# Where the load buffers of a one-token attention kernel start in SBUF, and which queue loads x

## The chip, the cores and the metric

The kernel runs on one core of one Trainium2 chip. The metric is device time in microseconds (us) of that core. A time is the median of several executions; nearly all executions of one kernel here agree within 0.1%. Each run of an experiment was timed beside executions of the kernel before on the same chip.

## The reference, cut to what matters

One token x of 640 values goes through a layer norm, a query projection, attention over a cache of 32,768 positions in 32 heads of 192, an output projection and a small ReLU MLP, all in bf16:

```python
q = (ln(x) @ wq).reshape(1, 1, 32, 192)           # wq: 640 x 6144
scores = einsum("bhqd,bhkd->bhqk", q, k_cache) * 192 ** -0.5
o = einsum("bhqk,bhkd->bhqd", softmax(scores), v_cache)
h = x + o.reshape(1, 1, 6144) @ wo                # then h + MLP(ln(h))
```

Keys and values are 403 MB each. Every byte is used once, so the kernel is a stream of loads with arithmetic beside it.

## The kernel before

SyncE issues every load. A key or value tile is 128 partitions with one contiguous row of 64 x 192 bf16 = 24,576 B each (3 MB in all); there are four key places and two value places, loaded in turn: key, value, key, value. A value load waits until PE has read the place (`PV`).

```python
def sbuf(name, shape, dtype):
    return ctx.enter_context(nc.sbuf_tensor(name, shape, dtype))
...
kt = [sbuf(f"kt{i}", [P, JL * Dh], bf16) for i in range(NL)]    # 4 x 24,576 B a partition
vt = [sbuf(f"vt{i}", [P, JL * Dh], bf16) for i in range(NV)]    # 2 x 24,576 B
wq_s = sbuf("wq_s", [P, DT * QG * Dh], bf16)                    # 15,360 B, rows of 3,072 B
wq_h = sbuf("wq_h", [P, DT, Dh], bf16)
wo_s = sbuf("wo_s", [P, 3, D], bf16)                            # rows of 3,840 B
...
def dma_program(g):                                             # SyncE
    ...
    load(x_row[:], A_x.rearrange("b s (c p) -> (b s c) p", p=P), "dx", "x")
    load(wq_v, wq_view[:, :, 0:QG * Dh], "dwq", "wq", 0)
    for h in range(H):
        for ld in range(NL if h < LAST else NL - 1):
            n = NL * h + ld
            load(kt[ld][:], rows(k_hd, h, P * JL * ld, JL), f"dk{ld}", "k", h, ld)
            if n >= NV:
                hp, lp = divmod(n - NV, NL)
                g.wait("PV", hp, 2 * lp + 1)
            load(vt[ld % NV][:], rows(v_hd, h, P * JL * ld, JL), f"dv{ld % NV}", "v", h, ld)
            # wq for the next eight heads, wo for the next two: at some h, ld
            ...
```

The allocator gives addresses in order, so each tile starts where the one before it ends.

The softmax here doesn't subtract the row's maximum and nothing guards it: scores larger than these inputs give would overflow.

## Time and profile before

| | |
|---|---|
| time | 1944.24 us (3 runs, 1944.11 to 1944.43) |
| span of the profiled run | 1941.3 us |
| bytes read from HBM | 825 MB |

The page cuts the span into 40 slices. A row of digits gives the busy share in each, in tenths, and the row GB/s gives what the 16 DMA engines moved. The trace also holds one record for each DMA packet, with its size and the time that it took. In this kernel a packet is one row of one partition; an engine serves 8 of the 128 rows of a load. These records are read from the trace file itself, since the usual views show only their sums. The *usual time* of a size is the time that the most packets of that size take; a packet that takes longer is called *late*.

### The profile page before, as it was taken

How to read it: one execution, taken by the hardware profiler on the slowest of the kernel's cores; microseconds unless marked ns; L12 is line 12 of the kernel's file. 1: busy time of each engine (PE TensorE's matmuls, PEld its weight loads, DVE VectorE, ACT ScalarE, POOL GpSimd, SP SyncE). 2: the span in 40 equal slices, each digit the busy share in tenths (PEclk: the TensorE clock that was granted, in tenths of full speed). 3: DMA queues.
4: the chain of work that ended last, by engine and by line, in shares of the span. 5: the costliest groups of instructions: out<-in, count | busy, mean ns of one | idle time of the engine just before them, and what ended most of it. 6: DMA issues, size and time to landing. Idle time of an engine off the chain costs nothing.

```text
span 1941.3 us, 36397 instructions
## 1 busy us (share of the span) xinstructions
PE 1601.3 (82%) x16098; PEld 1112.5 (57%) x16098; DVE 1590.4 (82%) x924; ACT 998.3 (51%) x2064; POOL 0.7 (0%) x6
## 2 busy tenths in 40 slices
PE   5887888787887888887788878888888888888887
PEld 3555555555555565655556556555555556565555
DVE  6888888887888888887888878888778888888886
ACT  4555545554455555455455555545445555554544
POOL 0000000000000000000000000000000000000000
PEclk9889889888898888888888988888888888888988
DMA  9999999999999999999999999999999999999997
GB/s 403 428 429 431 430 429 431 430 429 431 429 431 429 432 429 431 431 430 428 427 429 430 429 428 429 431 428 430 426 420 432 429 429 431 426 430 427 430 427 299
DMA packets 44814, 825.44 MB, mean 425 GB/s; under 512 B 4580, under 2 KB 6116, under 8 KB 12132
## 3 DMA queue, kind: packets, MB, share of 16 engines
q1 hardware_dynamic: 44772, 824.99, 99.6%
q8 instruction: 13, 0.21, 0.0%
q14 instruction: 29, 0.24, 0.0%
HBM read 824.97 MB, written 0.00 MB: 425 GB/s over the span
## 4 chain that ended last, share of the span: by engine, by line
DMA 76%; PE 22%; SPq 1%; issue 1%; ACT 0%; DVE 0%; POOLq 0%
DMA kt<-in_A_k_cache_dram 76%; PE o_ps L303 11%; PE tp L322 10%; SPq L210 1%; PE mm L303 1%; PE sp L303 0%; ACT kT L509 0%; POOLq L285 0%; DVE o_pair L620 0%; PE attT L303 0%; ACT pB L515 0%; PE mm L498 0%; ACT sd_ln L549 0%; DVE xn_ln L641 0%; DVE y_row L671 0%
## 5 line engine op out<-in xcount | busy, mean ns | idle before, releaser
L602 DVE TENSOR_TENSOR pr<-kt,qb 128x1536 f32<-128x1536 bf16 (+1 forms) x384 | 775.3, 2019 | 273.1 <-DMA kt<-in_A_k_cache_dram 259.1
L509 ACT COPY kT<-tp 128x1024 bf16<-128x1024 bf16 (+1 forms) x900 | 819.4, 990 | 324.0 <-PE tp L322 322.8
L322 PE MATMUL tp<-ident_f,kt 128*128 128x128 f32 x3462 | 572.0, 332 | 309.3 <-POOLq L285 308.9
L605 DVE TENSOR_REDUCE sc<-pr 128x8 f32<-128x1536 f32 (+1 forms) x384 | 773.9, 2015 | 13.3
L322 PEld LDWEIGHTS tp<-ident_f,kt 128*128 128x128 f32 x3462 | 498.7, 173 | 326.4 <-POOLq L285 324.3
L303 PE MATMUL o_ps<-vt,pB 128*2 128x384 bf16 x2286 | 468.1, 356 | 5.9 <-POOLq L285 5.9
L303 PE MATMUL o_ps<-vt,pA 128*2 128x384 bf16 x1778 | 330.8, 326 | 0.0
L303 PEld LDWEIGHTS o_ps<-vt,pB 128*2 128x2 bf16 x2286 | 183.4, 89 | 240.8 <-issue 82.4
L515 ACT ACTIVATE pB<-sp 128x20 bf16<-128x20 f32 (+2 forms) x258 | 48.1, 186 | 481.4 <-PE sp L303 481.4
L303 PEld LDWEIGHTS sp<-qm,kT 128*128 128x128 bf16 x6924 | 193.4, 97 | 83.6 <-issue 59.2
L303 PEld LDWEIGHTS o_ps<-vt,pA 128*2 128x2 bf16 x1778 | 150.6, 85 | 144.6 <-issue 7.9
L303 PE MATMUL sp<-qm,kT 128*128 128x2 bf16 x6924 | 212.1, 164 | 7.4 <-ACT kT L509 2.7
L524 ACT ACTIVATE pA<-sc 128x12 bf16<-128x12 f32 (+2 forms) x257 | 53.5, 208 | 113.6 <-DVE sc L605 112.2
L515 ACT ACTIVATION_READ_ACCUMULATOR pB<-sp 128x1 f32 x258 | 50.2, 195 | 0.0
L524 ACT ACTIVATION_READ_ACCUMULATOR pA<-sc 128x1 f32 x257 | 48.7, 190 | 0.0
L303 PE MATMUL mm<-ident_f,o_pair 2*128 2x1 f32 x384 | 47.8, 247 | 1.0 <-DVE o_pair L620 1.0
L303 PEld LDWEIGHTS mm<-ident_f,o_pair 2*128 2x128 f32 x384 | 45.1, 186 | 1.9 <-DVE o_pair L620 1.4
L610 DVE TENSOR_REDUCE rec<-mm 128x1 f32<-128x20 f32 x32 | 5.7, 179 | 46.3 <-PE mm L303 45.2
L532 ACT COPY wq_h<-wq_s 128x960 bf16<-128x960 bf16 x32 | 31.4, 980 | 2.9 <-DMA wq_s<-in_A_wq_dram 2.9
L620 DVE TENSOR_SCALAR o_pair<-o_ps,rec 2x384 f32<-2x384 f32 x32 | 28.4, 889 | 2.8 <-PE o_ps L303 1.7
L303 PE MATMUL mm<-wq_h,xn_ln 128*1 128x192 bf16 x160 | 18.7, 248 | 4.8 <-ACT wq_h L532 4.8
L303 PE MATMUL attT<-oT,wo_s 128*128 128x1 bf16 x465 | 15.9, 163 | 0.3 <-DVE oT L625 0.3
(65 smaller groups left out, 150.7 us busy)
## 6 DMA issues: line engine op xcount, KB each, us to landing
kt<-in_A_k_cache_dram SPq DMA_DIRECT2D x127, 3072.0 KB, 22.7
vt<-in_A_v_cache_dram SPq DMA_DIRECT2D x127, 3072.0 KB, 15.7
wq_s<-in_A_wq_dram SPq DMA_DIRECT2D x4, 1920.0 KB, 20.3
wo_s<-in_A_wo_dram SPq DMA_DIRECT2D x16, 480.0 KB, 17.0
kt<-in_A_k_cache_dram SPq DMA_DIRECT2D x1, 1920.0 KB, 19.9
kt<-in_A_v_cache_dram SPq DMA_DIRECT2D x2, 960.0 KB, 24.6
kt<-in_B_w_dram SPq DMA_DIRECT2D x1, 1920.0 KB, 20.3
wq_s<-in_B_w_dram SPq DMA_DIRECT2D x1, 960.0 KB, 22.2
```

What stands on the lines that cost most here:

```text
L210: g.do(lambda: nc.sync.dma_start(out=dst, in_=src), sem, label, by=16)
L303: return lambda: pe.matmul(o, lhsT=w, rhs=r, **kw)
L322: calls.append(lambda b=b, o=o: pe.transpose(out=dst[:, b, :], in_=src[:, o:o + 2 * P].bitcast(f32), identity=ident_f[:]))
L509: g.do(lambda: act.copy(out=kT[c % 2][:, b0:b0 + nb, :], in_=src[:, 0:nb, :].bitcast(bf16)), "act_pe", ("cp", h, c, k))
L515: g.do(lambda: act.activation(out=pB[c % 4][:, 0:jp], in_=sp[:, 0:jp], func=F.Exp, scale=SCALE, accum_out=dsums[:, 2 * c + 1:2 * c + 2]), ...
L524: g.do(lambda: act.activation(out=pA[c % 4][:, 0:jd], in_=sc[c % 4][:, 0:jd], func=F.Exp, scale=SCALE, accum_out=dsums[:, 2 * c:2 * c + 1] ...
L532: g.do(lambda: act.copy(out=wq_h[:], in_=wq_v[:, :, hh * Dh:(hh + 1) * Dh]), "act_pe", ("wqh", h))
L602: g.chain(lambda: dve.tensor_tensor(out=pr[:, 0:j1 - j0, :], in0=src[:, (off + j0) * Dh:(off + j1) * Dh].rearrange("p (j d) -> p j d", d=D ...
L605: red = lambda: dve.reduce_sum(out=sc[c % 4][:, j0:j1], in_=pr[:, 0:j1 - j0, :], axis=X)
L610: g.chain(lambda: dve.reduce_sum(out=rec[:, 0:1], in_=mm[:, 0:2 * NCM], axis=X), "dve_act")
L620: g.do(lambda: dve.tensor_scalar_mul(out=dst, in0=src, scalar1=rec[0:2, 1:2]), "dve_pe", ("os", h))
```

## The change

The intent: let the long rows land at multiples of 512 B, so that no row starts or ends within a block, and take the small load of x out of SyncE's queue so that the stream starts earlier.

```diff
-    def sbuf(name, shape, dtype):
-        return ctx.enter_context(nc.sbuf_tensor(name, shape, dtype))
+    def sbuf(name, shape, dtype, align=32):
+        return ctx.enter_context(nc.sbuf_tensor(name, shape, dtype, align_bytes=align))
@@
-    kt = [sbuf(f"kt{i}", [P, JL * Dh], bf16) for i in range(NL)]
-    vt = [sbuf(f"vt{i}", [P, JL * Dh], bf16) for i in range(NV)]
-    wq_s = sbuf("wq_s", [P, DT * QG * Dh], bf16)
+    kt = [sbuf(f"kt{i}", [P, JL * Dh], bf16, 512) for i in range(NL)]
+    vt = [sbuf(f"vt{i}", [P, JL * Dh], bf16, 512) for i in range(NV)]
+    wq_s = sbuf("wq_s", [P, DT * QG * Dh], bf16, 512)
     wq_h = sbuf("wq_h", [P, DT, Dh], bf16)
-    wo_s = sbuf("wo_s", [P, 3, D], bf16)
+    wo_s = sbuf("wo_s", [P, 3, D], bf16, 512)
@@ dma_program
-        load(x_row[:], A_x.rearrange("b s (c p) -> (b s c) p", p=P), "dx", "x")
@@ act_program
+        g.do(lambda: act.dma_start(out=x_row[:], in_=A_x.rearrange("b s (c p) -> (b s c) p", p=P)), "dx", ("x",), by=16)
```

## The prediction

> **What bounds the kernel now.** I read the slices and the queue table of the page first, to see whether one unit is full all the time.
>
> ```profile
> DMA  9999999999999999999999999999999999999997
> GB/s 403 428 429 431 430 429 431 430 429 431 429 431 429 432 429 431 431 430 428 427 429 430 429 428 429 431 428 430 426 420 432 429 429 431 426 430 427 430 427 299
> DMA packets 44814, 825.44 MB, mean 425 GB/s; under 512 B 4580, under 2 KB 6116, under 8 KB 12132
> q1 hardware_dynamic: 44772, 824.99, 99.6%
> ...
> DMA 76%; PE 22%; SPq 1%; issue 1%; ACT 0%; DVE 0%; POOLq 0%
> ```
>
> The 16 DMA engines are full in every slice but the last, and one queue, SyncE's, does 99.6% of it. The rate stands at 426 to 432 GB/s from slice 2 to slice 39, with one dip to 420. PE and VectorE are each busy for 82% of the span; they wait for data. Next came the stretches, to rule out a stage with another limit, and then the queue's own waits, because the chain of waits gives PE 22% and that had to be understood.
>
> ```profile
> 250.00:500.00 250.00, 205.73 (x2028) 143.15 (x2028) 204.64 (x115) 128.19 (x265) 0.00 (x0) 0.86 1.01 430
> 500.00:1000.00 500.00, 416.35 (x4181) 289.90 (x4181) 415.69 (x238) 257.12 (x533) 0.00 (x0) 0.87 1.00 430
> 1000.00:1500.00 500.00, 414.61 (x4156) 287.73 (x4155) 412.32 (x233) 258.31 (x536) 0.00 (x0) 0.88 1.00 429
> 1900.00:1941.00 41.00, 32.99 (x412) 23.58 (x412) 24.20 (x26) 18.52 (x43) 0.00 (x0) 0.83 0.70 278
> ```
>
> ```profile
> SPq L210 <- PE o_ps L303: 1343.1, 95, 33.9
> SPq L210 <- PE mm L303: 454.4, 31, 18.2
> ```
>
> SyncE's sequencer waits for PE for 1343 us in all (a value buffer must be read before it is filled again), yet the DMA share of the stretches stays 1.00. So these waits are back-pressure, not lost time: a 3 MB value load takes 7.3 us of the engines (3,145,728 bytes at 430 GB/s) and lands 15.7 us after its issue (median of the page's issue table), so some 8.4 us of work are still queued ahead of it when it goes out. The 22% of PE in the chain are the stretches in which the chain steps through such a release; no faster PE would shorten them.
>
> Last came the two ends, from the timeline and the chain in order of time.
>
> ```profile
> 0.96 0.38 SPq L210 DMA_DIRECT2D x_row<-in_A_x_dram  x1
> 1.40 0.40 SPq L210 DMA_DIRECT2D wq_s<-in_A_wq_dram  x1
> ...
> 8.90 0.99 ACT L532 COPY wq_h<-wq_s 128x960 bf16<-128x960 bf16 x1 [2.86 <-DMA wq_s<-in_A_wq_dram]
> ...
> 12.06 0.32 ACT L540 CAST qb<-mm 128x192 bf16<-128x192 f32 x1 [0.72 <-PE mm L303]
> 16.21 2.56 DVE L602 TENSOR_TENSOR pr<-kt,qb 128x2304 f32<-128x2304 bf16 x1 [9.65 <-DMA kt<-in_A_k_cache_dram]
> ```
>
> ```profile
> 1892.02 19.93 DMA kt<-in_A_k_cache_dram
> 1911.95 0.04 issue
> 1911.99 1.20 PE tp L322 x9
> ```
>
> At the start, [...]the query is ready at 12.4 us, 3.8 us before the first key tile lands. At the end, the last key pieces are waited for at 1912 us; from there to 1938 us the chain is compute on PE, ScalarE and VectorE, which no placement of buffers shortens. So the span is the stream of loads up to 1912 us, plus about 29 us.
>
> **What the Trainium skill says.** (1) "DMA: Bandwidth & Descriptors", section "Where 436 GB/s comes from": 16 ports of 32 B at 850 MHz are 435.2 GB/s. The trace runs at 430, which agrees and leaves 1.2% at the very most to win in the stream. (2) The same page, "How a descriptor splits into AXI transactions": a descriptor that doesn't start at a multiple of 256 B gets one more transaction, and the bytes skipped in the first one still cost 32-byte beats. This is the one statement that gives the change a mechanism; the trace speaks against its costing anything here, see below. (3) The same page, "Issuing engines are not separate DMA queues": issuing from several engines saves only the sequencer's time to issue. The trace has that time: 0.44 us. (4) "SBUF — State Buffer", "Operand start alignment" says that element-aligned places are legal and that its runs timed nothing; so it gives no speed either way.
>
> **The change part by part.**
> *Where things lie.* A 16,384-byte scratch and four 32-byte constants come first, so kt0 lies at byte 16,512 = 32 x 512 + 128. A kt or vt place is 24,576 B = 48 x 512, so all six places and wq_s (163,968) lie at 128 past a multiple of 512 (and of 256). After wq_s come 1,920 B of wq_h, which put wo_s at 181,248 = 354 x 512: wo_s is at a multiple of 512 already. After the change all are. The parts of the last head inside kt0 and kt1 start at multiples of 512 within their tile, so they follow. HBM rows of keys and values are 24,576 B long and contiguous, and don't change. That wo_s is aligned before is luck: it is a control inside the present trace.
>
> *What alignment could save.* From the trace's packet records (size and time taken), the usual time of a packet of each size is: 1,280 B 55 ns, 3,072 B 121, 6,144 B 234, 7,680 B 291, 15,360 B 573, 24,576 B 912; these all go to misaligned places. The wo rows, 3,840 B, to an aligned one: 149 (1,935 of 2,048 packets). By the skill's figure a beat is 1/0.85 = 1.18 ns. Packets minus their bare beats leave: 55-47.1 = 7.9, 121-112.9 = 8.1, 234-225.9 = 8.1, 291-282.4 = 8.6, 573-564.7 = 8.3, 912-903.5 = 8.5 ns misaligned; and 149-141.2 = 7.8 ns aligned. If the shift by 128 B cost 4 beats (4.7 ns), the aligned packet should leave about 3.5 ns. It leaves what the others leave, within 0.1 to 0.8 ns. So I take alignment to be worth 0 ns a packet in the main case. The check of scale: 8 packets of 912 ns and a semaphore write of 9 ns make 7.31 us a load, 430 GB/s, which is the plateau; packets run back to back and this is the whole cost.
>
> *x on the ScalarE queue.* SyncE drops one issue: 1.40 - 0.96 = 0.44 us earlier for wq and everything after, if ScalarE's issue doesn't hold up SyncE's. The stream is full from there to the end, so the shift arrives whole at the end: 0.44 us. ScalarE gains an issue of about 0.4 us before its first table load (0.91 to 2.19 now); its next work is at 5.74, so this is hidden. x itself is five packets of 256 B, 15 ns each.
>
> Sum: 1944.24 - 0 - 0.44 = 1943.8. Allowing the smaller chance of a gain its weight, I say 1943.5.
>
> **The rivals.**
> *A. The skill's beats are real at the write side.* Each of the 32,512 packets of 24,576 B saves 4.7 ns: 32,512 x 4.7 / 16 = 9.6 us; the smaller misaligned packets (3,456 + 256 + 256 + 128, and up to 1,536 of 1,280 B) add 4,096 x 4.7 / 16 = 1.2 to 1.7 us. With x: 1944.2 - 11.5 = 1932.8, 0.6% faster. For it: the cost of misalignment is stated on a page, and the room (8.5 ns over bare beats a packet, 17.3 us in all) is there. Against it: the aligned wo rows. The control isn't perfect, since 3,840 is 7.5 x 512 and a half block at its end may cost what the others lose by their start. I give A, or a part of it over 0.3%, 13%.
> *B. The time is in the stragglers.* The 24,576 B packets average 917.7 ns, not 912; the longest took 2,724 ns. The surplus over 912 is 11.5 us of the engines' time. If writes to whole 512 B blocks thin the stragglers, some of this comes back: 2 to 6 us. Nothing in the profile ties stragglers to a place, and a cause at the HBM side is as good; 7%, partly inside A.
> *C. A second queue costs something.* The two issues could be served one after the other, and then the 0.44 us shrink to nothing; x could also land late. The query has 3.8 us of slack, so lateness is hidden. Time: 1944.2. Added set-up for another queue might make 1944.5 to 1945.
> *D. A faster stream meets PE.* Only if A holds: PE and VectorE at 82% have room for 0.6%, so no new bound.
>
> **Range and chances.** Main case with and without C: 1943.4 to 1944.6, about four in five. A full A lies outside the range I give, a half A or B inside it: 1937 to 1945. More than 2% faster would need 39 us, more than twice the 17.3 us that packets spend beyond bare beats; more than 2% slower would need packets of 930 ns for no reason that I see. Faster 1%, within 2% 98%, slower 1%.
>
> **What would show it right or wrong.** The usual packet of 24,576 B: 912 ns means no effect, 907 means A. The plateau: 430 means none, 432 to 433 means A. The wo packet should stay at 149. The first wq issue should stand near 0.96 instead of 1.40 us, with x issued by ScalarE's sequencer beside it; the first key wait should end near 15.8 us instead of 16.2. The tail from the last key wait to the end should stay 29 us. The prediction is wrong if aligned long packets are faster than 910 ns, if the stragglers' 11.5 us fall by half, or if the stream shows a gap.

## The result, and the profile after

The changed kernel takes 1933.82 us (4 runs, 1932.93 to 1934.0) against 1944.17 us of the kernel before (4 runs, 1943.9 to 1944.43). The ratio is 0.9946, with a 95% interval of 0.9929 to 0.9963. That is 0.5% or 10.3 us faster: far within the 2% that count as "same", and outside the range that I gave (1937 to 1945).

The slices, queues and the chain of waits of the changed kernel, from its page:

```profile
DMA  9999999999999999999999999999999999999997
GB/s 404 432 431 434 432 432 433 432 431 434 431 433 432 433 432 432 433 432 431 433 432 432 433 430 432 432 430 426 429 432 433 430 429 432 429 427 428 433 431 298
q1 hardware_dynamic: 44762, 824.99, 99.6%
...
q10 hardware_dynamic: 10, 0.00, 0.0%
...
DMA 76%; PE 22%; SPq 1%; issue 0%; ACT 0%; DVE 0%; POOLq 0%
```

The kernel is bound by the same thing as before: DMA full, PE 22% of the chain. The plateau moved from about 430 to about 432 GB/s. The stretches (length; busy us and count of PE, its weight loads, VectorE, ScalarE, GpSimd; granted clock, DMA share, GB/s) say the same:

```profile
250.00:500.00 250.00, 206.06 (x2063) 144.04 (x2064) 204.80 (x118) 128.06 (x267) 0.00 (x0) 0.86 1.01 432
500.00:1000.00 500.00, 420.71 (x4189) 292.17 (x4188) 417.86 (x237) 259.27 (x537) 0.00 (x0) 0.87 1.00 432
1000.00:1500.00 500.00, 415.57 (x4202) 288.13 (x4201) 416.40 (x235) 262.64 (x541) 0.00 (x0) 0.89 1.00 431
```

SyncE's waits for PE are as long as they were, as back-pressure has to be:

```profile
SPq L210 <- PE o_ps L302: 1327.7, 95, 34.0
```

The two ends, from the timeline of the changed kernel:

```profile
0.91 0.56 ACTq L552 DMA_DIRECT2D x_row<-in_A_x_dram  x1
...
0.97 0.45 SPq L210 DMA_DIRECT2D wq_s<-in_A_wq_dram  x1
...
15.96 2.56 DVE L602 TENSOR_TENSOR pr<-kt,qb 128x2304 f32<-128x2304 bf16 x1 [9.40 <-DMA kt<-in_A_k_cache_dram]
```

```profile
1902.65 1.18 PE L321 MATMUL tp<-ident_f,kt 128*128 128x128 f32 x9
```

wq goes out 0.43 us earlier, and the first key is worked on 0.25 us earlier. The transposes of the last key pieces, which started at 1911.99 us, start at 1902.65; from there to the end of the span it is 29.1 us, after 29.3 before. So the time came out of the stream.

The packet records say where. For each kernel, over its 32,512 packets of 24,576 B: the share at exactly 912 ns; the mean; what the packets take above 912 ns, summed over all and divided by 16 engines, once for those up to 40 ns late (the *spread*) and once for those more than 40 ns late (the *stragglers*, with their number); and the time of all packets of the loads over 16 engines.

```
             at 912   mean ns   spread us   stragglers, us    all loads us
before        0.43     917.7      5.50        324, 6.05          1930.3
after         0.99     913.7      0.06        162, 3.40          1921.2
```

The usual packet didn't change: 912 ns. But before, only 43% of them took it; 56% took 913 to 929 ns, and 1% longer. After, 99% take 912. The same is true of the short rows: 1,280 B takes 55 ns in 33% of the packets before and in all of them after; 3,072 B takes 121 ns in 39% and in 99%. All packets together fall by 9.1 us: 5.4 from the spread of the long ones, 2.7 from their stragglers, 1.0 from the shorter rows. The stream starts 0.39 us earlier (its first packet at 2.08 instead of 2.46 us). Together that is 9.5 of the 9.6 us by which the span of the profiled runs fell.

### The profile page after: what moved, and what is told of

It is laid out like the page before. It is cut to its first block, busy times and chain, and to the rows that moved or that the text cites. A ratio compares the mean times of both kernels' runs of the same rounds, so it can differ in the third digit from the quotient of the medians.

```text
span 1931.7 us, 36397 instructions
## 1 busy us (share of the span) xinstructions
PE 1602.2 (83%) x16098; PEld 1113.3 (58%) x16098; DVE 1590.0 (82%) x924; ACT 998.5 (52%) x2064; POOL 0.7 (0%) x6
## 4 chain that ended last, share of the span: by engine, by line
DMA 76%; PE 22%; SPq 1%; issue 0%; ACT 0%; DVE 0%; POOLq 0%
DMA kt<-in_A_k_cache_dram 76%; PE o_ps L302 11%; PE tp L321 10%; SPq L210 1%; PE mm L302 1%; PE sp L302 0%; ACT kT L508 0%; POOLq L284 0%; DVE o_pair L620 0%; PE attT L302 0%; ACT pB L514 0%; PE mm L497 0%; ACT sd_ln L548 0%; DVE xn_ln L641 0%; DVE y_row L671 0%
```

## The experiments

Eleven kernels ran. The table has the packets of nine of them; the sections explain them. "Offset" is the start of the key and value rows past a multiple of 512 B. "Loads alone" are kernels that do nothing but load and then write zeros, so their output is wrong. Two more of these, dma_runs (1921.60 us) and dma_offsets (1926.79 us), change the offset on the way and have their own section.

```
             start of keys, values (mod 512)   at 912   mean ns   spread us   stragglers, us   time us   same chip, before
x_only        128                                0.40     917.8      5.71        271, 6.14      1943.48     1944.11
align_only    0                                  0.99     914.0      0.10        194, 3.98      1933.80     1944.11
off256        256                                0.99     913.6      0.11        181, 3.14      1934.22     1944.11
off32         32                                 0.13     919.4      8.32        310, 6.72      1947.61     1944.11
off64         64                                 0.21     918.1      6.49        317, 5.94      1945.70     1943.66
keys_only     keys 0, values 128                 0.97     914.5      0.28        269, 4.71      1935.06     1943.66
page4k        0 (mod 4096)                       0.99     913.7      0.08        145, 3.34      1933.32     1944.19
dma_off128    128, loads alone                   0.20     915.5      7.03          2, 0.05      1928.37     1943.66
dma_off0      0, loads alone                     1.00     912.1      0.03         13, 0.08      1919.13     1943.66
```

After the first look at the trace I held that the placement does it, by removing the spread (theory P), against the shift by the second queue (rival X) and the skill's extra beats, whose mark, a usual packet of 907 ns, the trace lacked.

### x_only: the queue alone

```diff
 # kernel before
-        load(x_row[:], A_x...., "dx", "x")                        # SyncE
+        g.do(lambda: act.dma_start(out=x_row[:], in_=A_x....), "dx", ("x",), by=16)   # first in act_program
```

> Only x moves to the ScalarE queue; all places stay at 128 past a multiple of 512 B. Theory P (placement makes the gain, by taking away the spread of 0 to 14 ns that two thirds of the misaligned packets show above their usual time): 1943.8 us, 0.4 us faster than before at most; the share of 24,576 B packets at exactly 912 ns stays near 0.43. Rival X (the shift of the stream by the second queue makes the gain): near 1934 us, share near 0.99.

It took 1943.48 us against 1944.11; ratio 0.9997 (0.9984 to 1.0011). The spread stayed. The medians differ by 0.6 us; the interval holds zero and ends at 3 us, far from 10. Rival X falls. (The "two thirds" of the expectation is too high: 57% of the long packets were late before.)

### align_only: the placement alone

```diff
 # changed kernel
+        load(x_row[:], A_x...., "dx", "x")                        # back on SyncE, first
-        g.do(lambda: act.dma_start(out=x_row[:], ...), "dx", ("x",), by=16)
```

> Only the places move to multiples of 512 B; x stays first on the SyncE queue. Theory P: 1934.2 us, that is the changed kernel plus 0.2 to 0.4 us, with the share of 24,576 B packets at 912 ns near 0.99 and their usual time still 912, not 907. Rival X: near 1944 us. If the skill's beats were the cause, the usual time would be 907 ns; after the changed kernel's trace I expect that no more.

It took 1933.80 us; ratio 0.9948 (0.9934 to 0.9962), the whole effect, with a usual packet of 912 ns. Theory P stands. The gap to the changed kernel (1933.82, another chip) is nothing, so x on ScalarE doesn't show beside it.

### off256 and off32: which boundary, and how the cost grows

```diff
 # kernel before
+    sbuf("pad", [P, 64], bf16)        # off256: 128 B; off32: 416 B
     kt = [sbuf(f"kt{i}", [P, JL * Dh], bf16) for i in range(NL)]
```

> All places moved by 128 B, so keys, values and wq start at 256 past a multiple of 512, and wo at 128; x on SyncE. Theory P256 (the boundary that counts is 256 B, the size of the transactions that the skill names): as align_only, 1934.5 us, share of long packets at 912 ns near 0.99; the wo packets, now at 128, lose their uniform 149 ns (share from 0.95 or 1.00 to about 0.4), worth 0.4 us. Theory P512 (the boundary is 512 B): as before, 1944 us, share near 0.43.

> All places moved by 416 B, so keys, values and wq start at 32 past a multiple of 512, wo at 416; x on SyncE. Theory E (any start off the boundary costs the same, a partial piece at each end of the row): as before, 1944 us, share at 912 ns near 0.43, spread worth about 2.7 ns a packet. Theory B (the cost is the extra 32-byte beats: 4 at offset 128, 1 at offset 32): a quarter of the spread, 0.7 ns a packet, 1936 to 1937 us.

Offset 256 took 1934.22 us (ratio 0.9949, 0.9936 to 0.9963), the same as offset 0, so the boundary that counts is 256 B and not 512. The stretches of the run with offset 256 and of the run with offset 32:

```profile
500.00:1000.00 500.00, 418.18 (x4226) 289.99 (x4224) 418.20 (x239) 259.11 (x539) 0.00 (x0) 0.88 1.00 432
```

```profile
500.00:1000.00 500.00, 420.09 (x4193) 291.68 (x4191) 414.77 (x237) 257.79 (x535) 0.00 (x0) 0.87 1.00 429
```

Offset 32 is the slowest of all: 1947.61 us (1.0019, 1.0005 to 1.0033). Its usual packet takes 915 ns, and its spread is 8.3 us where offset 128 has 5.5. Counting skipped beats, it should have cost a quarter. So theory B, the prediction's rival A in another form, falls, though it had named nearly the right time; and theory E, the same cost for every offset, falls too.

One part of the expectation for offset 256 failed in an instructive way. The wo rows lay at 128 there and were to lose their uniform 149 ns. 2,047 of the 2,048 took 149 ns, and one 156 (the expectation of keys_only below says all). A misaligned row among aligned ones costs nothing that the records show. In the kernel before, the aligned wo rows among misaligned neighbours were late in 5.5% of the cases; in the loads alone below, 114 of the 128 late ones are in the first quarter of their load. Lateness seems to be carried from one load into the next.

### dma_off128 and dma_off0: are the engines needed for it?

```diff
 # kernel before; dma_off0 has a pad of 384 B ahead of kt
+                if h > 0:
+                    g.wait("k", h - 1, ld)        # the load that filled the place before
...
-                    g.wait("PV", hp, 2 * lp + 1)
+                    g.wait("v", hp, lp)
 # and so on for wq, wo and the last head; programs of PE, ScalarE, GpSimd left out;
 # VectorE writes a zero row as output: wrong on purpose
```

> The same loads to the same places as the kernel before (128 past a multiple of 512 B), each waiting only for the load that filled its place before; no other engine does anything, and the output is zeros, wrong on purpose. Theory I (the spread arises in the transfer itself, at the partial piece at each row's edge): the share of 24,576 B packets at 912 ns stays near 0.43 and the mean near 917; about 1936 us, 10 us over the aligned twin. Theory C (the spread arises where misaligned writes meet the reads and writes of PE, VectorE and ScalarE in SBUF): share near 0.99, mean near 913, and the same time as the aligned twin, about 1927 us.

> The aligned twin of the loads alone: all places of keys, values and wq at multiples of 512 B. Both theories: share at 912 ns near 0.99, mean 913 to 914, about 1926 to 1927 us (the last load lands near 1922 us as in the aligned kernel, and then only the output is written).

1928.37 against 1919.13 us: 9.2 us apart with no engine at work, where 10 was expected of theory I. The middle stretch of each, offset 128 and then offset 0 (busy us of VectorE and GpSimd, clock, DMA share, GB/s):

```profile
500.00:1000.00 500.00, 0.00 (x0) 0.00 (x0) 1.00 1.00 430
```

```profile
500.00:1000.00 500.00, 0.00 (x0) 0.00 (x0) 1.00 1.01 432
```

The spread is a matter of the transfer itself; theory C, a meeting with the engines' reads, falls. The starts of the loads say the same without the packets' durations: in the middle (median) a load starts 7.272 us after the one before it at offset 0 and 7.303 us at offset 128, which over 254 loads is some 8 of the 9.2 us. I missed the level of both by 8 us. What is gone is the stragglers: 2 and 13 packets instead of 324 and 162. So the stragglers go with the engines' programs, and the spread doesn't. The spread is even larger here (7.0 us against 5.5; 20% of the packets take 912 ns where theory I expected 43%, and the most take 916). Why it is larger wasn't tested.

### keys_only: every second load misaligned

```diff
 # changed kernel
-    vt = [sbuf(f"vt{i}", [P, JL * Dh], bf16, 512) for i in range(NV)]
+    sbuf("pad", [P, 64], bf16)
+    vt = [sbuf(f"vt{i}", [P, JL * Dh], bf16) for i in range(NV)]      # at 128
```

> As the changed kernel (x on ScalarE), but the two value places stay at 128 past a multiple of 512 B; keys, wq and wo aligned. If each misaligned packet pays by itself: half of the effect, 1938.5 to 1939 us, share of all 24,576 B packets at 912 ns near 0.71. If the cost needs a run of misaligned packets behind one another (the wo packets at 128 in the run with offset 256 kept 149 ns, all 2,048 of them): less than half, under 1937 us, share over 0.8.

It took 1935.06 us; ratio 0.9956 (0.9942 to 0.9969). With half of the packets misaligned, 8.6 of about 10 us are there already, and 97% of all packets take 912 ns. Its middle stretch:

```profile
500.00:1000.00 500.00, 419.53 (x4177) 290.67 (x4178) 416.04 (x236) 257.26 (x533) 0.00 (x0) 0.87 1.00 432
```

So a misaligned packet doesn't pay its full cost by itself. That needs misaligned packets behind one another.

### off64

```diff
 # kernel before
+    sbuf("pad", [P, 224], bf16)       # 448 B
```

> All places moved by 448 B: keys, values and wq start at 64 past a multiple of 512 B, wo at 448; x on SyncE. If the cost grows as the common divisor of start and 256 shrinks (offset 128 had a mean of 917.7 ns, offset 32 919.4): between the two, usual time 912 to 915 ns, 1944 to 1947.5 us. If offset 32 is a case of its own, below a 64 B line: as offset 128, usual time 912, 1944 us.

1945.70 us; 1.0008 (0.9994 to 1.0022). The usual packet takes 914 ns: between offsets 128 and 32.

### dma_runs and dma_offsets: how long a run, how far off

Both are the loads alone, with places 512 B longer, so that each load can start where it likes:

```diff
 # dma_off0
-    load(kt[ld][:], rows(k_hd, ...), ...)
+    load(kt[ld][:, place(2 * n):place(2 * n) + JL * Dh], rows(k_hd, ...), ...)   # values: 2 * n + 1
 # dma_runs:    place(i) is 0 for i // r even, else 128 or 32 B; r = 1, 2, 4, 8 loads
 # dma_offsets: place(i) changes every 16 loads
```

> Loads alone, output zeros on purpose. Of every pair of runs of loads, one run goes to aligned and one to misaligned places, so half of all packets are misaligned throughout; the run's length changes: 1, 2, 4, 8 loads at offset 128, then 1, 2, 4 at offset 32, then one head all at 32. Theory Q (the write side is slower than the read side by a few ns for misaligned packets and faster for aligned ones, with a queue between; a packet is late only once the queue is full): mean surplus of all packets near 0.1 ns at length 1, rising with the length towards half of the full 3.5 ns, 1.7, at length 8; and late packets stand at the end of a misaligned run, with some carry into the first aligned ones. Theory S (each misaligned packet pays by itself): 1.7 ns at every length.

> Loads alone, output zeros on purpose. The start of the key and value rows changes every two heads (2,048 packets of 24,576 B each): 0, 128, 256, 64, 192, 32, 224, 96, 160, 16, 240, 4, 2, 128, 0 bytes past a multiple of 512. Theory B (skipped 32-byte beats cost): surplus over 912 ns rises with the offset, 32 least (1 beat), 128 four times that, 224 seven times. Theory D (what counts is the largest power of two that divides the start: 128, then 64, then 32): 128 about 3.5 ns, 64 and 192 alike about 4, 32, 224, 96 and 160 alike about 5 ns, 16 and 240 alike and at least as much, 4 and 2 more; 0 and 256 none.

Mean surplus over 912 ns of the packets of each load within one period, for runs of 8 aligned loads and then 8 at offset 128 (three periods averaged), and for 4 and 4 at offset 32:

```
8 and 8, offset 128:  0.5 0 0 0 0 0 0 0 | 0 0 0 0.8 2.4 2.4 3.1 3.6
4 and 4, offset 32:   1.2 0 0 0 | 0 0 3.3 4.7
mean over all packets: offset 128, runs of 1, 2, 4, 8: 0.3 0.5 0.5 0.8;  offset 32, runs of 1, 2, 4: 1.1 0.8 1.2;  all at 32: 4.6
```

This fits theory Q. After eight aligned loads, the first 24 misaligned packets of each engine (three loads of 8) take 912 ns like aligned ones. Then lateness sets in, grows to its full size, and is carried into the first aligned load after it. (In two of the three periods the fifth load is at full size already; in the third, the aligned wq is reloaded, lateness starts only in the seventh, and that bends the averages.) So something in each engine, called the *store* from here on, takes up the slower writing until it is full, and is drained while aligned packets pass. It is inferred; no record shows it directly.

Its size can only be estimated. After eight aligned loads, lateness at offset 128 starts after some 28 packets, and after the 16 aligned ones at the start of dma_offsets after some 36; at 3.6 ns each, that is 100 to 130 ns. After only four aligned loads it starts after some 22 packets at offset 128 and some 18 at offset 32 (4.7 ns each), 80 to 85 ns in both cases. By the same estimate that is what 32 aligned packets make room for, some 2.6 ns each. It would explain why even runs of one load cost something: 8 misaligned packets fill in more than 8 aligned ones drain.

Theory S, each packet pays by itself, falls: it needed 1.7 ns at every length. Theory Q had the shape right and missed both ends: 0.3 ns at length 1 (0.8 in the last of its four heads, once the store had filled), not 0.1, and 0.8 at length 8, not 1.7, since three of the eight loads pass before anything shows.

Of the offsets, each with 2,048 packets, the loads after lateness has set in have these mean surpluses (left out: stragglers, the first load of a step, the pauses that follow a reload of the aligned wq, and the one load of each step beside the wo load, whose short rows lie at 384 in this kernel and which is 1 to 2 ns later):

```
offset     0    256   128       96, 160     64, 192     32, 224     16, 240   4     2
surplus    0    0     3.4-3.8   3.5-3.8     3.5-4.2     4.5-4.9     5.7-6.1   5.7-6.1  5.7-6.1
```

The values are symmetric: 224 costs what 32 does, 240 what 16 does. Beats skipped (1 for offset 32, 7 for 224) don't explain it, and neither does the largest power of two alone, which would put 96 and 160 beside 32 (theories B and D). The numbers go by the distance to the nearest multiple of 256 B, and the cost falls as it grows: 5.7 to 6.1 ns at 16 B and less, 4.5 to 4.9 at 32, about 3.4 to 4.2 from 64 on. What exactly is counted stays open. Every offset tried but 256 costs 3.4 to 6.1 ns a packet once the store is full.

In the same run, the reload of wq (15,360 B a partition to an aligned place) brings two or three loads of keys and values back to 912 ns each of the three times: the drain at work, by chance.

### page4k: is more alignment better?

```diff
 # changed kernel: every 512 in the four allocations
-    ..., bf16, 512)
+    ..., bf16, 4096)
```

> The changed kernel with its places at multiples of 4,096 B instead of 512. The packets stand at 912 ns for 99% already, so nothing is left for the place to give: 1933.8 us, within 1 us of the changed kernel. Rival: if the stragglers (162 packets over 950 ns, 3.4 us in all) depend on the page, up to 3 us less.

1933.32 us (1933.11 to 1934.51; 0.9945, 0.9932 to 0.9959): the same as the changed kernel. None of the runs points to a version that is clearly faster than it.

## Why the prediction was wrong, point by point

**The bound** was right. The stream of loads fills the engines, the waits for PE are back-pressure, and the tail of 29 us stayed (29.1).

**The step that failed** is the one under "What alignment could save": "So I take alignment to be worth 0 ns a packet in the main case." I compared the usual time of each packet size, and the misaligned sizes left as much over bare beats as the aligned wo rows. The comparison was correct and it was the wrong quantity. In the full kernels the usual time is 912 ns at offset 0, 256 and 128 alike (at 64 and 32 it is 914 and 915). The cost of misalignment stands in the share of packets that leave it: in place of 0 ns, the mean of the long packets fell by 4.0 ns (917.7 to 913.7), and align_only gave the whole 10 us. The same control held that answer: 94% of the aligned wo packets were at their usual time, against 43% of the long misaligned ones and 33% of the 1,280 B rows. I gave "1,935 of 2,048" for wo and no such share for the others.

The prediction's check of scale (8 packets of 912 ns and a semaphore write make 7.31 us a load, "the whole cost") fitted by coincidence. Aligned loads have the same 912 ns and the same write, and start 7.272 us apart. So the durations in the records overlap by some 4 ns a packet, and the check couldn't show that the misaligned stream lost anything. For the same reason the room of 8.5 ns a packet was too large: 7,272 ns for eight packets leave 5.5 ns beyond the bare beats.

Of the prediction's own signs, the plateau of 432 GB/s ("means A") and the halved stragglers came, and the usual packet of 912 ns ("means no effect") came too. They contradict each other because the cost is not where the last of them looks.

**Rival B** ("the time is in the stragglers") had the right place, the surplus of 11.5 us over 912 ns, and was mis-sized: it allowed 2 to 6 us, at 7%. The surplus fell by 8.1 us, from 11.5 to 3.5, and the shorter rows gave 1.0 more. It also ran together two things that the runs separate: a spread up to 40 ns, which is 5.5 us and there in the transfers alone, and real stragglers, 6.0 us, which all but vanish without the engines' programs.

**Rival A** named 1932.8 us, 1 us from the result, and by its own mark it was false: the usual packet is 912 ns, not 907. Offset 32 (one extra beat) costs more than offset 128 (four), and offset 224 costs the same as 32. The number was right by coincidence. (The prediction's citation, "gets one more transaction", holds on its page for rows like these, multiples of 256 B; the page's own misaligned example of 96 B gets none more.)

**x on ScalarE** was worth 0.4 us in the sum. wq did go out 0.43 us earlier and ScalarE's issue was hidden, but in the times it shows as 0.6 us in one comparison and as nothing in the other, both inside the noise. Unresolved, and too small to matter. **Rival C**, its cost, didn't appear.

**What stays open.** Aligned full kernels have 145 to 194 stragglers, kernels with all long rows misaligned 271 to 324, and that difference is worth some 2 to 3 us of the 10. They all but vanish in the loads alone, but those also fetch fewer instructions (15 or 16 packets on the instruction queues instead of 55), so the two aren't separated. Of those in the kernel before, 54 of 324 lie within 3 us of a packet that fetches instructions, on a queue of the same DMA engines; most of the others come after 1100 us. In the changed kernel 53 of 162 do, so alignment thins the others alone, from 270 to 109. Why it does wasn't tested. That the store sits between an engine's read and write side fits the runs, and is inferred.

## What to carry to other kernels

When a stream of long loads is the bound, start its rows at multiples of 256 B in SBUF; it costs a few hundred bytes and here gave 0.5%. If only some tiles can be aligned, interleave aligned and misaligned loads: here half of the placement gave over 80% of the effect. And when you read packet or instruction records, look at the share at the usual time and at the mean, not at the usual time alone: a cost that is stored up and paid by some moves the distribution and leaves its peak where it was.

## What the Trainium skill lacked or had wrong

- "DMA: Bandwidth & Descriptors", section "How a descriptor splits into AXI transactions": its boundary of 256 B agrees with the runs (offset 256: 1934.22 us, offset 0: 1933.80, offset 128: 1944.11). The page words its count of beats for reads and doesn't say whether it holds for writes to SBUF, which the runs varied. For these it isn't the cost: offsets 32 and 224, 1 and 7 extra beats by that count, both cost 4.5 to 4.9 ns a packet, and 128, with 4, costs 3.4 to 3.8.
- The same page lacks that the cost is hidden at first: after eight aligned loads, at least 24 misaligned packets of 24,576 B an engine, at offset 128, pass at 912 ns before any is late, and alternating aligned loads hide nearly all of it (97% at 912 ns).
- "SBUF — State Buffer", section "Operand start alignment", says that its runs timed nothing; here the start of DMA rows moves the time from 1933.8 us (offset 0) through 1944.1 (128) to 1947.6 (32).
- "DMA: Bandwidth & Descriptors", section "Why small descriptors are slow (HBM only)", gives about 3 cycles of overhead a packet; at 850 MHz that is an estimate of 3.5 ns. The records here last 7.8 to 8.6 ns beyond the bare beats, for rows of 1,280 to 24,576 B, but overlap: by the starts of aligned loads (7.272 us for eight packets and a semaphore write) it is 5.5 ns, that write included. No run takes these 5.5 ns apart.
- "SBUF — State Buffer", section "Who interferes with whom", says that DMA never contends with a compute engine. The spread agrees, since it is there without the engines (7.0 us against 5.5). The stragglers are not explained: 324 (aligned 162) of 32,512 packets more than 40 ns late with the engines at work, 2 and 13 in the loads alone. Fetches of instructions by DMA, which the loads alone lack too, lie near 54 of the 324.
